# A forward-and-backward adaLN block on one Trainium2 core: the 2048-point transform split as 16 x 128 instead of 128 x 16

## The chip, the cores and the metric

The kernel runs on one core of a Trainium2 chip. The metric is the device time of one launch in microseconds (us); lower is better. The engines are TensorE (PE; its weight loads are listed apart as PEld), VectorE (DVE), ScalarE (ACT), GpSimd (POOL) and SyncE (SP). DMAs are issued from SP's queue and from POOL's.

## The reference

The block computes an output and the gradients of all its inputs but one, for 2048 rows of width 576 in bfloat16:

```
mod = silu(c) @ w_mod                     # sa, ca, ga, sb, cb, gb, 576 each
h = layernorm(x) * (1 + ca) + sa
X = rfft2(h)                              # over 2048 rows and 576 columns, 289 frequencies kept
y = irfft2(X * (w_r + 1j * w_i))
x = x + ga * y
h = layernorm(x) * (1 + cb) + sb
x = x + gb * (((h @ w_gate) * (h @ w_up)) @ w_down)     # hidden width 4608
# outputs: x, and the vjp for grad_out: x, w_r, w_i, w_gate, w_up, w_down, c, w_mod
```

The two-dimensional transform is needed once forward (h to y) and once backward (gradient of y to gradient of h, with the filter's gradient from both spectra).

## The kernel before

The 2048 rows are cut into 16 blocks of 128, row 16 p + t in partition p of block t. The columns' transform is a product with a table (RD forward, RF on folded rows backward). The transform of 2048 rows is split: within a block over the 128 partitions with the twiddled table G1, then across the 16 blocks.

**Head, first stage** (`s1_norm`, `s1_cols`, `s1_rows`; three steps of a software pipeline over the blocks). A block is normalised, transposed on PE (five products of 128 columns, L473), multiplied by the scaled table RDs (ten of 292, L482) and by G1 (four of 292, L502 and L503), and its planes are copied to VA. Meanwhile grad_out is transposed on PE (L532) and scaled by DVE into goT (L535).

**Head, second stage** (`s2_*`, 19 chunks of up to four groups out of 73). A group holds four frequencies of all 16 blocks. For each group PE transposes it (L599), multiplies with BD2, the 16-point transform as a block-diagonal table (L607), DVE multiplies by the filter wn (L238) and adds, PE transposes back (L628) and multiplies with BDA (L636). ACT and DVE copy each result out of PSUM. Between the steps `u4_groups` puts two groups of the ghh product (`u4_group`, L572: five matmuls of 512 columns each, 144 groups in all), and the last three modulators (`mod_make`).

**Head, third stage** (`s3_*`, 16 blocks). `rows_back` (L210, L212) multiplies the planes with the twiddled table GB, `cols_back` (L217) with IF, the halves are folded (L219 to L221), the residual and the second norm follow. Three groups of ghh go between, the rest after.

**Middle.** The gated products forward and backward and the weight gradients, over 36 hidden blocks (L757, L840, L879).

**Tail, first stage** (`t1_*`, 16 blocks): backward through the second norm, a PE transpose (L1166), twelve narrow matmuls for the modulators' diagonals (`diag`, L1053), six with RF (L1181) and four with G1 (L1188, L1189). **Second stage** (`t2_*`): the same 19 chunks as in the head. **Third stage** (`t3_*`): `rows_back`, `cols_back`, the first norm backward. `filter_grad` forms the filter's gradient from the kept spectrum Xn on DVE (L1290 to L1295), `product_rows` the rows of the w_mod gradient (L1095).

The order on PE in the tail is written out by hand. `staged` keeps the matmuls of every step; `deal` puts a fixed number `q` of other matmuls behind each step: the last weight gradients (`held`) and the first five pairs of output tiles (`proj`, L1464), 896 in all, and ties the whole into one chain with `in_order`. ACT's order in the first tail stage, and ACT's and DVE's in the third, are tied likewise. In the head a planner orders the work by priorities and costs. PSUM has eight banks: in the head five for `fps` and three for `u4ps`; in the tail three for `ps_fp`, three single ones for `ps_cs` (csA, csB, csC) and two for `ps_u3`. An engine takes its instructions in order, so one that waits holds all behind it.

## Time and profile before

| | us |
|---|---|
| median of 3 runs | 1499.98 |
| lowest and highest | 1499.88, 1500.52 |
| profiled execution | 1497.33 |
| its span | 1495.6 |
| PE busy | 1476.1 (99%) |
| DVE busy | 1057.9 (71%) |
| ACT busy | 566.9 (38%) |
| POOL busy | 255.0 (17%) |
| granted TensorE clock, mean | 0.998 |

The profile is one execution. A line of a group names the kernel's line, the engine, the operation, output and inputs by tile, the shapes and the count; then the busy time and the mean duration in ns of one; then the idle time of the engine just before these instructions and what ended most of it. A line of the timeline starts with its start in us and its length. Matmuls are pipelined and their ends are modelled, so that a row of ten lasts from its start to the start of the next row.

### The profile page before, as it was taken

What the parts mean: (1) busy time and instruction counts of PE and PEld (TensorE: products, weight loads), DVE (VectorE), ACT (ScalarE), POOL (GpSimd) and SP (SyncE); (2) the same over time, 40 slices, a digit from 0 to 9 for tenths busy, and PEclk for the clock granted to TensorE, in tenths of its full rate; (3) what the DMA queues carried; (4) which work ended last, traced back from release to release, by engine and by line L of the source; (5) the groups of instructions that cost most, each with busy time, mean ns of one, the idle gap of its engine ahead of it and who ended that gap; (6) DMA issues with size and microseconds to landing.
All of it is one profiled execution on the core that took longest, in us unless ns stands there. A gap on an engine that the chain in (4) does not pass through costs nothing.

```text
span 1495.6 us, 29166 instructions
## 1 busy us (share of the span) xinstructions
PE 1476.1 (99%) x11249; PEld 1009.5 (68%) x11251; DVE 1057.9 (71%) x2648; ACT 566.9 (38%) x1186; POOL 255.0 (17%) x396
## 2 busy tenths in 40 slices
...
GB/s 323 274 224 212 241 224 187 155 152 168 161 138 181 138 127 180 134 139 183 128 143 185 117 146 177 124 150 174 124 155 142 132 141 295 266 262 193 245 312 149
DMA packets 486350, 272.92 MB, mean 182 GB/s; under 512 B 413921, under 2 KB 457186, under 8 KB 485186
## 3 DMA queue, kind: packets, MB, share of 16 engines
...
## 4 chain that ended last, share of the span: by engine, by line
PE 91%; DMA 3%; issue 2%; DVE 2%; POOL 1%; SPq 1%; ACT 0%; POOLq 0%; DVEq 0%; ACTq 0%
PE u57p L757 27%; PE u8p L879 19%; PE gup L840 17%; PE u4p L572 10%; PE u3p L1464 5%; PE gup L835 3%; PE yp L217 1%; PE u57p L791 1%; DMA gonA<-in_grad_out_dram 1%; DMA h2p<-in_A_x_dram 1%; PE zp L1181 1%; PE upa L210 1%; PE zp L482 1%; DMA gxc<-gx_d 1%; PE u4p L567 0%
## 5 line engine op out<-in xcount | busy, mean ns | idle before, releaser
L884 DVE TENSOR_TENSOR acc<-acc,u8p 128x288 f32<-128x288 f32 (+1 forms) x1088 | 483.0, 452 | 276.2 <-PE u8p L879 272.5
L879 PE MATMUL u8p<-wT,ggT 128*128 128x288 bf16 x1152 | 327.8, 286 | 0.7 <-DVE acc L884 0.7
L879 PE MATMUL u8p<-wT,guT 128*128 128x288 bf16 x1152 | 327.5, 286 | 0.0
L840 PE MATMUL gup<-h2T,wgu 128*128 128x512 bf16 x1152 | 297.8, 379 | 0.0
L759 ACT CAST so<-u57p 128x288 bf16<-128x288 f32 x208 | 82.9, 399 | 510.9 <-PE u57p L757 505.3
L757 PE MATMUL u57p<-h2p,gu_sf 128*128 128x288 bf16 x1088 | 176.6, 286 | 0.0
L757 PE MATMUL u57p<-h2p,gg_sf 128*128 128x288 bf16 x1088 | 176.6, 286 | 0.0
L840 PEld LDWEIGHTS <-wgu 128*128 128x128 bf16 x1152 | 109.6, 98 | 97.9 <-issue 17.1
L879 PEld LDWEIGHTS <-ggT 128*128 128x128 bf16 x1152 | 112.6, 98 | 66.9 <-issue 14.5
L572 PE MATMUL u4p<-goT,wdT 128*128 128x512 bf16 x668 | 153.8, 379 | 0.0
L879 PEld LDWEIGHTS <-guT 128*128 128x128 bf16 x1152 | 112.7, 98 | 56.1 <-issue 0.9
L1464 PE MATMUL u3p<-wd,hl 128*128 128x288 bf16 x936 | 140.1, 286 | 0.5 <-ACT ob L1469 0.5
L842 ACT CAST gT<-gup 128x512 bf16<-128x512 f32 x144 | 84.4, 586 | 131.5 <-PE gup L840 129.6
L757 PEld LDWEIGHTS <-hh_sf 128*128 128x128 bf16 x1152 | 112.7, 98 | 28.4
L1464 PEld LDWEIGHTS <-hl 128*128 128x128 bf16 x1152 | 107.5, 98 | 26.6 <-issue 3.4
L757 PEld LDWEIGHTS <-gu_sf 128*128 128x128 bf16 x1088 | 106.5, 98 | 27.0
L757 PEld LDWEIGHTS <-gg_sf 128*128 128x128 bf16 x1088 | 106.5, 98 | 26.8
L842 ACT CAST uT<-gup 128x512 bf16<-128x512 f32 x144 | 84.4, 586 | 77.5 <-PE gup L840 77.5
L572 PEld LDWEIGHTS <-wdT 128*128 128x128 bf16 x668 | 62.5, 98 | 70.9 <-issue 5.5
L757 PE MATMUL u57p<-gonC,hh_sf 128*128 128x288 bf16 x576 | 99.7, 286 | 0.0
L855 POOL DMA_DIRECT2D hhT_d<-hhT x36 | 33.2, 923 | 373.8 <-DVE hhT L844 373.2
L169 ACT CAST ghh_st<-u4p 128x512 bf16<-128x512 f32 x94 | 53.7, 589 | 53.6 <-PE u4p L572 52.9
...
## 6 DMA issues: line engine op xcount, KB each, us to landing
...
```

The lines of the kernel that those rows point to most:

```text
L169: nc.scalar.copy(dst, src)
L210: nc.tensor.matmul(ps_a[:, fc, :], lhsT=A[:, c, sa, 128 * fc:128 * fc + 128], rhs=GB[:, sa, 1 - c:3 - c, :].rearrange("k v s -> k (v s)"), ...
L572: nc.tensor.matmul(pt[:], lhsT=wdTs[k][:, j, m, :], rhs=goT[:, 4 * sb4:4 * sb4 + 4, m, :], start=(m == 0 and n == 5), stop=(m == n - 1))
L757: mm = nc.tensor.matmul(pw[0][:, 0:288], lhsT=sf[:, t, :], rhs=rhs_n(t, h * 288, 288), start=(t == 0), stop=(t == NT - 1))
L759: followed(mm, nc.scalar.copy(so[:, h * 288:(h + 1) * 288], pw[0][:, 0:288]))
L835: nc.tensor.matmul(pts[-1][:], lhsT=wgu[r, 8, jw * 128:(jw + 1) * 128], rhs=h2T[r, 4 * sb4:4 * sb4 + 4, 4, :], start=True, stop=False)
L840: nc.tensor.matmul(pts[k][:], lhsT=wgu[:, 4 * wi_ + m, jw * 128:(jw + 1) * 128], rhs=h2T[:, ts_, m, :], start=False, stop=(m == 3))
L842: nc.scalar.copy((gT, uT)[wi_][:, th_, :], pts[k][:])
L855: nc.gpsimd.dma_start(hhT_d[:, :, fb, :].rearrange("tp f x -> f tp x"), hhT[:].rearrange("f (tp ti) p -> f tp (ti p)", ti=2))
L879: nc.tensor.matmul(pu[:, 0:288], lhsT=l_, rhs=r_, start=(k == 0), stop=(k == len(mms) - 1))
L884: summed[t] = nc.vector.tensor_tensor(out=ghb(t)[:, hs_] if fbs[-1] == NFB - 1 else dst, in0=dst, in1=pu[:, 0:288], op=ADD).ins
L1464: mm = nc.tensor.matmul(p2[ti][:, 0:288], lhsT=hls[fb // 9][:, fb % 9, ti * 128:(ti + 1) * 128], rhs=w[:, fb - f0, h * 288:(h + 1) * 288], ...
```

## The change

The split is turned round: 16 points first, within one turned block, then 128 points.

- The turn of a block is a matmul with the table F16 in place of the identity (`turn16`): it turns the block and takes the 16-point transform of it at once. The result goes to h2T (head) or GY (tail), real and imaginary lanes side by side. The 73 group turns and products with BD2, and those back with BDA, are gone, and VA, Vp and the planes A with them.
- Lanes i and 16 - i are made as a pair (eight pairs, the last holding lanes 0 and 8). `freq_rows` takes four results of two matmuls each from the pair's columns with G1, `both_signs` makes both lanes from their sums and differences (two copies on ACT, four DVE operations), `spectral_product` multiplies by the filter and forms sums and differences again, `plane_back` goes back over 128 points with GB.
- `cols_back` now comes before `rows_back`, which is a matmul with I16 (F16 transposed) on each half.
- The column part (RD, RF) moves from the first stages into the second. The head's first stage keeps the norm, the turn and grad_out's transposes; ghh groups, modulators and the turn of the first two w_down blocks on PE lie between them by a written order. The loads on SP are reordered; the turned half of the filters is read through a DRAM copy (back_d).
- In the tail `deal` gives 24, 12 and 17 matmuls a step (before 16, 12 and 16); the second norm's last affine and the product rows go from DVE to ACT; the filter gradient is taken by lane (16 in place of 19), eight of them in the third stage; G1, GB and I16 are loaded in the first stage; half of the filter gradient's store goes through a DRAM copy (gback_d).

```diff
+    p = 16 * (q % 8) + q // 8
+    th = 2 * np.pi * p[:, None, None] * (16 * k1[None, None, :] + k2[None, :, None]) / S
     G1 = np.stack([np.cos(th), -np.sin(th), np.sin(th)], axis=2)
-    thp = 2 * np.pi * (q[:, None, None] * (16 * k1[None, None, :] + t[None, :, None])) / S
+    thp = np.transpose(th, (2, 1, 0))
     GB = np.stack([-np.sin(thp), np.cos(thp), np.sin(thp)], axis=2)
...
+    F16 = np.zeros((128, 128), f8)
+    for j in range(NT):
+        kk = j // 2 if j > 1 else 8 * j
+        w = np.cos(2 * np.pi * np.arange(NT) * kk / NT) if j % 2 == 0 or j == 1 else -np.sin(2 * np.pi * np.arange(NT) * kk / NT)
+        for l in range(8):
+            F16[8 * np.arange(NT) + l, 8 * j + l] = w
...
+    def lane(i, u):
+
+        return i if u == 0 else NT - i if i else NPR
+    def turn16(src, dst, t, room, tag):
+        pts = [room.tile([128, 4, 128], FP32, name="tr16", tag=tag) for _ in range(2)]
+        for m in range(5):
+            mm = nc.tensor.matmul(pts[m // 4][:, m % 4, :], lhsT=src(m), rhs=T["F16"][:], start=True, stop=True)
+            if m > 2:
+                n = 4 if m == 3 else 1
+                followed(mm, nc.scalar.copy(dst[:, :, m + 1 - n:m + 1, 8 * t:8 * t + 8].rearrange("q j m l -> q m j l"), pts[m // 4][:, 0:n, :].rearrange("q m (j l) -> q m j l", l=8)))
+    def freq_rows(G, zt, i, new):
+        ps = [new() for _ in range(4)]
+        ar, ai, br, bi = (zt[:, a, c, :] for a in range(2) for c in range(2))
+        for p_, (k, terms) in zip(ps, ((i, ((0, ar), (2, br))), (i, ((0, bi), (1, ai))), (i, ((0, ai), (2, bi))), (i, ((0, br), (1, ar)))) if i else
+                                  ((0, ((0, ar), (2, ai))), (0, ((0, ai), (1, ar))), (NPR, ((0, br), (2, bi))), (NPR, ((0, bi), (1, br))))):
+            for n, (pl, z) in enumerate(terms):
+                nc.tensor.matmul(p_[:, 0:FP], lhsT=G[:, k, pl, :], rhs=z, start=(n == 0), stop=(n == 1))
+        return ps
+    def both_signs(ps, i, X, pool):
+        if i == 0:
+            for n, p_ in enumerate(ps):
+                nc.scalar.copy(X[:, n // 2, n % 2, :], p_[:, 0:FP])
             return
+        es = pool.tile([128, 2, FP], FP32, name="es", bufs=1)
+        for n in range(2):
+            nc.scalar.copy(es[:, n, :], ps[2 * n][:, 0:FP])
+            for u, op in ((n, SUB), (1 - n, ADD)):
+                nc.vector.tensor_tensor(out=X[:, u, n, :], in0=es[:, n, :], in1=ps[2 * n + 1][:, 0:FP], op=op)
+    def spectral_product(X, wn, i, sd, nrest, pool, conj):
+        m1 = pool.tile([128, 2, 2, 2, FP], BF, name="fm", bufs=1)
+        for c in range(2):
+            nc.vector.tensor_tensor(out=m1[:, c], in0=X, in1=wn[:, c, lane(i, 0):lane(i, 1) + 1:lane(i, 1) - lane(i, 0), :].unsqueeze(2).to_broadcast([128, 2, 2, FP]), op=MUL)
+        Y = m1[:, 0].rearrange("k u c f -> k (u c) f")
+        for c in range(2):
+            nc.vector.tensor_tensor(out=m1[:, 0, :, c, :], in0=m1[:, 0, :, c, :], in1=m1[:, 1, :, 1 - c, :], op=ADD if conj == (c == 0) else SUB)
+        for f0, w, at in ((0, FM, 0), (FM, FP - FM, 2 * FM)):
+            dst = [sd[:, e, at:at + 2 * (FM if at == 0 else 64)].rearrange("k (c f) -> k c f", c=2)[:, :, 0:w] for e in range(2)]
+            if i:
+                nc.vector.tensor_tensor(out=dst[0], in0=y[:, 0:2], in1=y[:, 2:4], op=ADD)
+                nc.vector.tensor_tensor(out=dst[1], in0=y[:, 1:3], in1=y[:, 3::-3], op=SUB)
...
+    def plane_back(GB, sd, i, nrest, ut, new):
         for fc in range(2):
+            ps = new()
+            for e in range(2):
+                for n in range(2):
+                    a, c, k = (n, e, i) if i else (e, n, NPR * e)
+                    nc.tensor.matmul(ps[:, 256 * e:256 * e + 256], lhsT=sd[:, a, FM * c + 128 * fc:FM * c + 128 * fc + 128], rhs=GB[:, k, 1 - n:3 - n, :].rearrange("k v s -> k (v s)"), start=(n == 0), stop=(n == 1))
...
+            for e in range(2):
+                nc.scalar.copy(dst[:, e], ps[:, 256 * e:256 * e + 256].rearrange("f (v s l) -> f v s l", v=2, l=8))
+        ps = new()
...
+        nc.scalar.copy(ut[:, 4, :, 16 * i:16 * i + 16].rearrange("f s (u l) -> f u s l", l=8), ps[:, 0:256].rearrange("f (u s l) -> f u s l", u=2, l=8))
+    def cols_back(ut, t, yps, IF, pool):
         for p_, pls in enumerate(((0, 2, 4), (1, 3, 4))):
             for k, pl in enumerate(pls):
+                nc.tensor.matmul(yps[p_][:, 0:DF], lhsT=ut[:, pl, t, :], rhs=IF[:, 3 * p_ + k, :], start=(k == 0), stop=(k == 2))
+            made.append(nc.scalar.copy(zz[:, p_, :], yps[p_][:, 0:DF]).ins)
+    def rows_back(zz, yps, I16, pool, out):
+        for p_ in range(2):
+            nc.tensor.matmul(yps[p_][:, 0:DF], lhsT=I16, rhs=zz[:, p_, :], start=True, stop=True)
...
-        PE_TURNED = (13, 15, 17)
+        PE_TURNED = (0, 1, 13, 15, 17)
...
+        T = {"F16": load_table(hp1, "F16")}
         x_load(0, 1)
-        wms[MCA] = mod_load(MCA)
-        T = {"RD": load_table(hp1, "RD", "tA")}
+        wms[MGB] = mod_load(MGB)
         go_load(0)
         wd_load(0)
+        x_load(4, 8)
+        go_load(1)
         x_load(8, 12)
         go_load(2)
         x_load(12, NT)
+        wms[MCA] = mod_load(MCA)
+        T["RD"] = load_table(hp1, "RD", "tA")
+        T["G1"] = load_table(hp1, "G1")
+        for c, filt in enumerate((wr_v, wi_v)):
+            nc.sync.dma_start(back_d[c].rearrange("k j f -> j k f"), turned_rows(filt))
...
+        gate()
+        s1_norm(0)
+        pe_turn(0)
+        s1_stats(1)
+        s1_stats(2)
+        for t in range(1, NT):
+            if t in (4, 6, 8, 12):
+                s1_stats(t)
+            s1_norm(t)
+            go_turn(t - 1)
+            if t == 5:
+                pe_turn(1)
+                mod_make(MGB, wms[MGB], "a")
+                wms[MSA] = mod_load(MSA)
+            if t == 13:
+                shift_row()
+            if t == 7:
+                scaled_table()
+            if t == 9:
+                mod_make(MCA, wms[MCA])
+                wd_ready(2)
+                wms[MGA] = mod_load(MGA)
+            if t in (4, 6, 8, 9, 10, 11, 12, 13, 14):
+                u4_groups(1)
+        go_turn(NT - 1)
+        nc.gpsimd.memset(wn[:, :, :, DF:FP], 0.0)
+        for c, filt in enumerate((wr_v, wi_v)):
+            nc.sync.dma_start(wn[:, c, 0:NPR + 1, 0:DF], filt[:, 0:NPR + 1, :])
+            nc.sync.dma_start(wn[:, c, NPR + 1:NT, 0:DF], back_d[c])
+        nc.gpsimd.dma_start(wn_d, wn[:].rearrange("k c a f -> k (c a f)"))
+        for k_ in ("GB", "I16"):
+            T[k_] = load_table(hp1, k_)
+        for j in (MGA, MSB, MCB):
+            u4_groups(2)
+            mod_make(j, wms.get(j) or mod_load(j), "a")
...
+                ps = freq_rows(T["G1"], zts[n], i, new)
+                X = Xs[n] = c2.tile([128, 2, 2, FP], BF, name="Xc")
+                both_signs(ps, i, X, c2)
+                nc.sync.dma_start(xn_d[:, i * W4:(i + 1) * W4], X[:].rearrange("k u c f -> k (u c f)"))
...
+            for k in range(NPR + 3):
+                if k > 2:
+                    s2_back(k - 3)
+                    u4_groups(1)
+                if 1 < k < NPR + 2:
+                    s2_filter(k - 2)
+                if 0 < k < NPR + 1:
+                    s2_rows(k - 1)
+                    u4_groups(1)
+                if k < NPR:
+                    s2_cols(k)
+                if k == 0 or k >= NPR:
+                    u4_groups(2)
+            in_order(pe_since(mark))
...
-        pipeline(NT, [lambda sa: (s3_rows(sa), u4_groups(3, "a")), s3_cols, s3_norm])
+        pipeline(NT, [lambda sa: (s3_cols(sa), u4_groups(3, "a")), s3_rows, s3_norm])
...
-            if name == "1":
-                nc.scalar.activation(out=part(w), in_=part(n), func=ACT.Identity, bias=ab[:, 0:1], scale=ab[:, 1:2])
-            else:
-                nc.vector.tensor_scalar(out=part(w), in0=part(n), scalar1=ab[:, 1:2], scalar2=ab[:, 0:1], op0=MUL, op1=ADD)
+            scaled["w" + name].append(nc.scalar.activation(out=part(w), in_=part(n), func=ACT.Identity, bias=ab[:, 0:1], scale=ab[:, 1:2]).ins)
...
-                q = 16 if stage == 1 else 12 if stage == 2 else 20 if k == 0 else 16
+                q = 24 if stage == 1 else 12 if stage == 2 else 20 if k == 0 else 17
...
-            nc.vector.tensor_scalar(out=o8[r, m, :], in0=d[r, :], scalar1=sc_col[r, m:m + 1], scalar2=None, op0=MUL)
+            nc.scalar.activation(out=o8[r, m, :], in_=d[r, :], func=ACT.Copy, scale=sc_col[r, m:m + 1])
...
+                        for tab, tag, at in (("RF", "tA", 10), ("G1", None, 11), ("GB", None, 13), ("I16", None, 14)):
+                            if t == at:
+                                T[tab] = load_table(tl0, tab, tag)
+                                in_order([ins.ins, tab_ins[tab]])
...
-                for m in range(5):
-                    mm = nc.tensor.transpose(pt[:, m, :], rings["gxf"][:, t % 3, wide(m)], ident[:])
+                turn16(lambda m: rings["gxf"][:, t % 3, wide(m)], GY, t, ps_fp, "fp")
...
-            steps = [t1_norm, t1_turn, t1_cols, t1_last]
+            steps = [t1_norm, t1_out, t1_turn, t1_last]
...
+        def filter_grad(g):
+            i, u, s_ = g // 2, g % 2, lane(g // 2, g % 2)
+            Xn = fg.tile([128, 2, FP], BF, name="Xn2")
...
+            for c in range(2):
+                nc.vector.scalar_tensor_tensor(out=t1[:, c], in0=Xn[:, c, :].unsqueeze(1).to_broadcast([128, 2, FP]), scalar=CSC, in1=gY(i)[:, u], op0=MUL, op1=MUL)
+            nc.vector.tensor_tensor(out=wn[:, 0, s_, :], in0=t1[:, 0, 0, :], in1=t1[:, 1, 1, :], op=ADD)
+            nc.vector.tensor_tensor(out=wn[:, 1, s_, :], in0=t1[:, 0, 1, :], in1=t1[:, 1, 0, :], op=SUB)
...
-            pipeline(NCH, [t2_turn, t2_filter, None, t2_back, t2_inv, t2_grad], 2)
+            def new_cs():
+                turn[0] += 1
+                return ps_cs.tile([128, 512], FP32, name="fq", tag="cs" + "ABC"[turn[0] % 3])
+                        for m in range(3):
+                            nc.tensor.matmul(zp[:, 0:FP], lhsT=GY[:, 2 * i + a, 2 * cc + m, :], rhs=T["RF"][:, 3 * cc + m, :], start=(m == 0), stop=(m == 2))
+                        nc.scalar.copy(zt[:, a, cc, :], zp[:, 0:FP])
+            def t2_rows(n):
+                both_signs(freq_rows(T["G1"], zts[n], pairs[n], new_cs), pairs[n], gY(pairs[n]), c2)
+            def t2_filter(n):
+                spectral_product(gY(pairs[n]), wn, pairs[n], sds[n % 2], nrest, c2, True)
+            def t2_back(n):
+                plane_back(T["GB"], sds[n % 2], pairs[n], nrest, utB, new)
+            pipeline(NPR, [t2_cols, t2_rows, t2_filter, t2_back], 2)
...
+        T["IF"] = load_table(tl0, "IF", "tA", nc.gpsimd)
...
-            ut = uts[sa] = c3.tile([128, 640], BF, name="ut", bufs=3)
-            own["ut", sa] = [nc.scalar.copy(ut[:, 0:512], upa[:].rearrange("f c s -> f (c s)")).ins, nc.scalar.copy(ut[:, 512:640], upb[:, 0:128]).ins]
-            ye, *own["fold", sa] = cols_back(uts[sa], [ps_fp.tile([128, 512], FP32, name="yp", tag="fp") for _ in range(2)], T["IF"], c3, ghr3[:, sa % 3, :])
+            ye, *own["fold", sa] = rows_back(zzs[sa], [ps_fp.tile([128, 512], FP32, name="yp", tag="fp"), ps_cs.tile([128, 512], FP32, name="yp", tag="csB")], T["I16"][:], c3, ghr3[:, sa % 3, :])
...
-            if sa in (4, 7, 10, 13):
-                filter_grad(rest[sa // 3 - 1])
+            if sa % 2:
+                filter_grad(rest[sa // 2])
...
-        pipeline(NT, [t3_rows, t3_cols, t3_norm, t3_sums], 3)
+        pipeline(NT, [t3_cols, t3_rows, t3_norm, t3_sums], 3)
...
-            for ci in rest[{9: 4, 10: 6, 11: 8}.get(t, 99):][:2]:
+            for ci in rest[{9: 8, 10: 12}.get(t, 99):][:4]:
...
+                    if t == 8:
+                        nc.gpsimd.dma_start(gback_d[c], wn[:, c, NPR + 1:NT, 0:DF])
+                    if t == 9:
+                        nc.gpsimd.dma_start(turned_rows(o_v), gback_d[c].rearrange("k j f -> j k f"))
+                if t == 11:
+                    scale_ends(0, NPR + 1)
+                for k in {11: range(2), 12: range(2, 4), 13: range(4, 6)}.get(t, ()):
+                    nc.gpsimd.dma_start((o2_v, o3_v)[k % 2][:, 3 * (k // 2):3 * (k // 2) + 3, :], wn[:, k % 2, 3 * (k // 2):3 * (k // 2) + 3, 0:DF])
 
```

500 lines of the change are left out of this document (167 added, 333 removed).

## The prediction

> **What bounds the kernel now.** I read the page first (busy time by engine), then the stage table for the stretches that the change touches, then TensorE's timeline inside them, and last the groups by line for durations on VectorE (DVE) and ScalarE (ACT).
>
> ```profile
> PE 1476.1 (99%) x11249; PEld 1009.5 (68%) x11251; DVE 1057.9 (71%) x2648; ACT 566.9 (38%) x1186; POOL 255.0 (17%) x396
> ```
>
> ```profile
> 0.00:14.00 14.00, 10.21 (x126) 8.98 (x126) 6.51 (x35) 7.00 (x12) 3.58 (x16) 1.00 0.80 268
> 14.00:16.00 2.00, 0.60 (x6) 0.60 (x7) 1.77 (x9) 1.16 (x2) 0.00 (x0) 0.86 0.99 392
> 16.00:18.00 2.00, 2.00 (x10) 1.08 (x9) 1.53 (x6) 1.50 (x2) 0.00 (x0) 0.50 1.06 392
> 18.00:20.00 2.00, 1.81 (x15) 1.17 (x13) 1.74 (x7) 1.73 (x5) 0.19 (x1) 0.78 1.06 384
> 20.00:64.20 44.20, 41.63 (x428) 31.89 (x427) 25.39 (x69) 30.55 (x77) 5.17 (x7) 1.00 0.97 312
> 64.20:130.30 66.10, 66.10 (x535) 40.02 (x533) 47.51 (x139) 42.89 (x86) 7.52 (x14) 1.00 0.71 213
> 1243.00:1313.50 70.50, 70.45 (x741) 58.18 (x740) 55.82 (x157) 56.27 (x134) 24.60 (x37) 1.00 0.88 284
> 1313.50:1367.70 54.20, 53.66 (x597) 45.78 (x595) 47.52 (x134) 43.81 (x93) 12.09 (x27) 1.00 0.59 193
> 1367.70:1432.20 64.50, 63.82 (x601) 52.24 (x601) 57.62 (x167) 46.92 (x111) 17.89 (x32) 1.00 0.81 255
> ```
>
> The columns are the stretch in us, its length, the busy time of PE, PEld, DVE, ACT and POOL, the granted clock, the DMA share and GB/s. Six rows are the stages in question: the forward transform's column part (to 64.2), its spectral part (to 130.3), then the three tail stages. In the last four PE is idle for 1.3 us in all. So TensorE is the bound wherever the change works, except before about 20 us, and a matmul taken away is time taken away as long as nothing else is late. The margins are thin: in the first tail stage DVE is busy for 55.82 and ACT for 56.27 of 70.50 us.
>
> PE's busy time is modelled, so I take prices from start to start.
>
> ```profile
> 114.00 0.39 PE L607 MATMUL xp<-T_BD,VT 128*128 128x128 bf16 x4
> ...
> 114.89 2.32 PE L572 MATMUL u4p<-goT,wdT 128*128 128x512 bf16 x10
> 117.05 0.39 PE L607 MATMUL xp<-T_BD,VT 128*128 128x128 bf16 x4
> ```
>
> ```profile
> 1286.83 0.44 PE L1166 MATMUL trp<-ident,gxf 128*128 128x128 bf16 x5
> ...
> 1287.63 1.14 PE L1464 MATMUL u3p<-wd,hl 128*128 128x288 bf16 x8
> 1288.61 0.29 PE L1188 MATMUL vp<-zt,T_G 128*128 128x292 bf16 x1
> ...
> 1289.11 0.65 PE L1464 MATMUL u3p<-wd,hl 128*128 128x288 bf16 x4
> ```
>
> ```profile
> 1417.15 0.60 PE L210 MATMUL upa<-T_GB,j_A 128*128 128x256 bf16 x4
> 1417.59 0.28 PE L212 MATMUL upb<-T_GB,j_At 128*128 128x128 bf16 x2
> 1417.70 0.65 PE L1464 MATMUL u3p<-wd,hl 128*128 128x288 bf16 x4
> ```
>
> One chunk of the spectral part is four groups of four narrow matmuls, 114.00 to 114.89: 0.89/16 = 0.056 us each. Ten of the ghh product's matmuls with 512 columns take 2.16 us, 0.216 each, so a group of five is 1.08. A fill matmul of 288 columns is 0.98/8 = 0.1225. Four of 292 columns take 0.50 (0.125 each). Five transposes with twelve diagonal matmuls take 0.80. Of 256 columns one is 0.11, of 128 again 0.055.
>
> **The change part by part: TensorE.** Removed: the turn, the 16-point product, the second turn and the second product of 73 column groups, so 4 x 73 = 292 narrow matmuls in each direction, 584 in all: 584 x 0.056 = 32.7 us. Added: two matmuls of 289 columns with the I16 table for each of 16 row blocks in each direction, 64 x 0.125 = 8.0 us. Two more blocks of w_down are turned on PE instead of by DMA: 20 x 0.056 = 1.1 us. Same count and width, only moved: the turn by F16 (five of 128 per block, as the transposes), the column part (160 and 96 of 292), the row part (64 of 292 each way), the way back (64 of 256 and 32 of 128, now 78 and 4, the same columns). Net: 8.0 + 1.1 - 32.7 = -23.6 us of PE work, of which the tail has -12.4 and the head -11.2 (4.0 + 1.1 - 16.4). The 20 warm-up matmuls at 12 us go too; they lay in a wait, so nothing. This is all gain only if no new wait appears.
>
> **Who takes over: durations.**
>
> ```profile
> L1290 DVE SCALAR_TENSOR_TENSOR gwt<-Xn,b_Vp 128x512 f32<-128x512 bf16 x36 | 24.2, 683 | 0.1
> ...
> L238 DVE TENSOR_TENSOR fm<-b_Vp,wn 128x512 bf16<-128x512 bf16 x36 | 13.6, 419 | 5.9 <-ACT b_Vp L1316 5.9
> ...
> L535 DVE TENSOR_TENSOR goT<-u4p,gbT 128x640 bf16<-128x640 bf16 x16 | 12.7, 815 | 14.0 <-PE u4p L532 14.0
> L181 DVE BATCH_NORM_STATS2 ln_st<-h2p 128x6 f32<-128x288 bf16 x32 | 12.7, 436 | 4.4 <-DMA h2p<-in_A_x_dram 4.4
> ...
> L220 DVE TENSOR_TENSOR ghr<-yp,ye 128x289 bf16<-128x289 f32 x16 | 7.3, 455 | 0.0
> ...
> L1322 DVE TENSOR_TENSOR Ygc<-fm 128x256 bf16<-128x256 bf16 x18 | 5.1, 285 | 0.3
> ```
>
> ```profile
> L1016 ACT ACTIVATE w<-n1c,ab 128x576 bf16<-128x576 bf16 x16 | 14.1, 881 | 0.3 <-DVE ab L1010 0.3
> ...
> L169 ACT COPY hT<-trp 128x640 bf16<-128x640 bf16 x16 | 11.1, 693 | 1.1 <-PE trp L473 1.1
> ...
> L1371 ACT CAST ut<-upa 128x512 bf16<-128x512 f32 x16 | 9.4, 589 | 9.2 <-PE upa L210 9.2
> ...
> L1371 ACT CAST ut<-upb 128x128 bf16<-128x128 f32 x16 | 4.4, 275 | 0.0
> ```
>
> Each row ends with busy us and mean ns. Neighbours overlap a little: 36 times 419 ns is 15.1 us, but the row was busy 13.6, so sums of means come out about 10% high. From 256 to 512 columns a bf16 product grows by 134 ns, 0.52 ns a column on a base of 0.15 us. A column pair then costs DVE: four signed sums from PSUM at 0.455 = 1.82; two products of 1168 columns at 0.76, two sums of 584 at 0.46, two of 512 at 0.42, two of 72 at 0.19 = 3.66; together 5.5 us, about 5.0 with the overlap. ACT: six copies of 292 columns (between 0.275 and 0.589, by width 0.41) and five of 256 (0.38) = 4.4 us.
>
> **Head, first stage.** With the column part gone from it, PE has here only 80 turns and 80 transposes of grad_out (9.0 us), two modulators and the shift row (30 matmuls of 288 to 292 columns, 3.7), the modulators' columns (80 matmuls of one column, an estimate of 2 to 4 from the 0.056 of 128), w_down (1.1) and nine ghh groups (9.7): some 26 us. So PE no longer sets its length. DVE does: it is busy 36.9 us to 64.2 (6.51 + 1.77 + 1.53 + 1.74 + 25.39), of which 25.4 are the statistics and the scaled copies of grad_out, which stay. What leaves is six plane copies of 292 columns (0.455 each by the row of ghr), six norms and two copies of ghh (0.4 to 0.6 each by the same rows), 6 us; what comes is four copies of w_down of 640 columns, 2 to 3 us at no more than goT's 0.794. That makes some 33 us. It starts at about 5 us and waits for x at times: the stage ends at 43. Six ghh groups and three modulators follow (6 x 1.08 + 3 x 1.23 = 10.2): 54 us is the lower end for the spectral part's start. The upper end is the DMA: by 64.2 us the queues have moved 0.268 x 14 + 0.392 x 4 + 0.384 x 2 + 0.312 x 44.2 = 19.9 MB, and the new order wants about as much before that point: x, grad_out, w_down, the filters and the stores of n1 as before; earlier than before GB (it was loaded after the spectral part) and three modulators; in addition a DRAM copy of the filters' turned half; but G1 and GB are 9/16 as large. At the measured rate that is 60 to 63 us. On SP's queue the last modulator's load stands behind the filter loads and GB, and the third modulator product waits for it. I take 58, between the ends, since the loads that PE needs first (x, grad_out) go out first now.
>
> **Head, spectral part.** A pair costs PE 28 x 0.125 + 10 x 0.11 = 4.6 us; with 24 ghh groups eight pairs make 62.7 us. A step with two ghh groups is 6.76; DVE needs 5.0 and ACT 4.4 of it, each and one ghh copy of 512 columns (0.59 by the row of ut): PE holds it. I add 2 us for the first and last pair. It ends at 58 + 65 = 123 against 130.3, with 39 ghh groups made instead of 42, 3.2 us still owed: -4.1. In the third stage each of 16 blocks costs 0.25 for I16 and no longer the 0.55 of the way back: -4.8. Head: -8.9, with ends -13 (start at 54) and -4 (at 63).
>
> **Tail.** The 896 fill matmuls (the last weight gradients and the first five output tile pairs, dealt between the steps, 109.8 us) stay; 16, 12 and 16 a step become 24, 12 and 17. First stage: a step is PE 0.80 + 24 x 0.1225 = 3.74 us in place of 4.01. ACT has two norms and w, moved there from DVE (576 columns, 0.88 each by the w row), two turn copies (0.59 + 0.275, formerly one of 0.693) and two thirds of a fill copy (0.27): 3.8 by means, 3.4 with overlap. So about 70 us as now, but 152 fills further. Second: eight pairs 28.8 + 132 fills 16.2 = 45.0 us of PE in place of 54.2; DVE at 5.0 of 5.07 us a pair has no slack, the last pair's way back must land before the next stage's first matmul, and the tail's row part has four results for three banks (csA, csB, csC): 3 to 8 us lost, I take 4. Third: 326 fills and 16 x (8 x 0.125 + 0.27) make 60.2 us of PE. ACT gets 20 product rows there, formerly DVE's, of 576 columns, so 0.88 us by the nearest row: w and u (0.88), ye and two zz (0.41) and half a fill copy are 3.2 a step, with these rows 16 x 3.2 + 17.6 = 69 us, 62 with overlap. DVE loses those rows but has eight filter gradients of 2 x 0.76 + 2 x 0.46 = 2.4 us instead of four. I take 2.5 us of loss, with 0 and 8 as ends. After it nothing changes: 432 output matmuls cover what is left, and the filter stores number ten instead of 16. Tail: -12.4 + 4 + 2.5 = -5.9, ends -12 and +4.
>
> **Sum.** The profiled execution took 1497.3 us, 1.7 more than its span, and 2.7 less than the median of 1499.98. 1497.3 - 8.9 - 5.9 = 1482.5 there, 1485 for the median.
>
> **The clock: row against rule.** From 14 to 16 us PE is idle for 1.4 of 2 us, and in the two after that the granted clock is 0.50. The new first stage gives PE 26 us of work in 43, in many short gaps. If it ran at half clock throughout, its 26 us would be 52, the spectral part would start at 5 + 52 + 10 = 67 instead of 58, and the time be 1494. The Trainium skill, "TensorE: Matmul & The Clock Gate", Part 1, says the clock falls to half after an idle window of about 3.4 us and rises after as long of sustained work. By that rule the short gaps would not lower it and the head's term stays as summed. The row is harsher than the rule: 1.4 us of idling in a stretch of two came before the fall.
>
> **The rivals.** (1) All of the PE work is gained, the new waits being covered: 1500 - 23.6 = 1476. For it: four stages with 1.3 us idle. Against it: the DVE and ACT sums above. (2) The gain is mostly eaten in two places, the late modulator in the head (-4) and ACT or DVE in the tail's third stage (-2): 1494. (3) The half clock in the head, also 1494, and 1501 if it lasts through the first pair (6.8 us more). (4) Slower: the pairs run at the pace of their own chain. Rows need four PSUM banks at once, freed only when DVE has made the signed sums, and PE takes its instructions in order, so a late bank holds the ghh and fill matmuls behind it. If the 1.82 us of sums stand bare in each of 16 pairs, that is 29 us: 1485 + 29 - 6 (the losses counted) = 1508. It decides from 1.3 us a pair on, (15 + 6)/16. Against it: now, too, each chunk passes PE, ACT, DVE, PE, ACT, PE, with idle of 0.5 us in 54.2.
>
> **How the numbers follow.** My case (1479 to 1491) 0.45, (1) 0.15, (2) 0.18, (3) 0.07, (4) 0.15. This kernel's measurement tells about 0.2%, 3 us, from no change. Faster: 0.45 + 0.15 + 0.13 of (2) and 0.03 of (3), 0.76; within it the rest of (2) and 0.03 of (3), 0.08; slower (4) and 0.01 of (3), 0.16. The range reaches from just under (1) to between (3) and (4): 1474 to 1503; my case's own is 1479 to 1491.
>
> **What would show it.** Right: no narrow 128-column groups in the spectral parts; pairs every 6.8 us in the head and 5.1 in the tail; the spectral part starting at 54 to 63 us. Wrong: PE idle released by DVE's signed sums or by the banks csA to csC, PE waiting on a modulator load near 55 us, a granted clock under 1 past 20 us, or ACT at 95% in the third tail stage with PE waiting for zz.

## The result and the profile after

The changed kernel takes 1552.49 us (median of four runs, 1549.55 to 1557.08) against 1499.93 before (1498.01 to 1500.52): 1.0355 times the time, 95% interval 1.0328 to 1.0383. The prediction was 1485, and the range 1474 to 1503 does not hold it. The profiled execution took 1549.55, its span is 1546.5, 50.9 more than before.

The first fence is the page's busy time by engine, the second the stage table of the changed kernel, cut at the same places as that of before; its columns are those of the prediction.

```profile
PE 1460.5 (94%) x10701; PEld 987.6 (64%) x10703; DVE 1049.7 (68%) x2576; ACT 558.7 (36%) x1191; POOL 248.4 (16%) x393
```

```profile
0.00:72.08 72.08, 49.69 (x451) 34.53 (x452) 34.81 (x116) 36.33 (x78) 10.51 (x27) 0.83 0.95 313
72.08:264.67 192.59, 191.55 (x1111) 102.16 (x1109) 121.55 (x281) 110.35 (x251) 30.18 (x57) 1.00 0.71 203
264.67:1255.67 991.00, 989.54 (x7106) 669.26 (x7106) 696.39 (x1651) 257.77 (x508) 140.15 (x187) 1.00 0.73 149
1255.67:1338.12 82.45, 66.59 (x689) 54.83 (x687) 44.37 (x133) 51.66 (x108) 19.48 (x40) 0.94 0.84 283
1338.12:1385.38 47.26, 46.32 (x377) 36.11 (x375) 40.87 (x107) 32.59 (x94) 5.96 (x11) 1.00 0.33 115
1385.38:1450.00 64.62, 55.39 (x483) 42.68 (x482) 55.90 (x151) 49.85 (x112) 16.36 (x29) 1.00 0.71 218
1450.00:1520.10 70.10, 61.37 (x498) 48.01 (x496) 44.36 (x117) 19.59 (x40) 16.53 (x28) 0.95 0.78 232
1520.10:1546.50 26.40, 0.02 (x1) 0.00 (x0) 11.47 (x26) 0.57 (x1) 9.22 (x16) 0.57 0.37 89
```

The rows of before that answer to these and were not shown yet:

```profile
0.00:64.20 64.20, 56.26 (x579) 43.73 (x580) 36.95 (x122) 41.93 (x96) 8.94 (x23) 0.97 0.94 310
64.20:259.47 195.27, 195.25 (x1260) 103.41 (x1257) 123.93 (x307) 115.75 (x234) 33.37 (x61) 1.00 0.79 220
259.47:1246.37 986.90, 985.95 (x7074) 666.13 (x7073) 694.88 (x1647) 255.85 (x504) 138.02 (x184) 1.00 0.76 151
1246.37:1313.50 67.13, 67.08 (x714) 55.58 (x713) 52.45 (x148) 55.87 (x133) 22.20 (x35) 1.00 0.86 285
1432.20:1488.70 56.50, 54.00 (x442) 42.66 (x439) 43.90 (x125) 6.22 (x16) 21.96 (x34) 1.00 0.81 252
1488.70:1495.60 6.90, 0.04 (x1) 0.00 (x0) 0.60 (x3) 0.57 (x1) 0.55 (x1) 0.84 0.19 40
```

Length less PE's busy time is PE's idle time, so the two tables (with the two tail rows in the prediction) give the whole account, in us:

| stretch | length before, after | PE busy, change | PE idle before, after |
|---|---|---|---|
| start to the first pair's column product | 64.2, 72.1 | -6.6 | 7.9, 22.4 |
| to the middle | 195.3, 192.6 | -3.7 | 0.0, 1.0 |
| middle, to the tail's first turn | 986.9, 991.0 | +3.6 | 1.0, 1.5 |
| first tail stage | 67.1, 82.5 | -0.5 | 0.1, 15.9 |
| second | 54.2, 47.3 | -7.3 | 0.5, 0.9 |
| third, and the outputs to PE's last matmul | 121.0, 134.7 | -1.1 | 3.2, 18.0 |
| after PE's last matmul | 6.9, 26.4 | 0 | 6.9, 26.4 |
| sum | 1495.6, 1546.5 | -15.6 | 19.5, 86.0 |

(The middle is 4 us longer because 32 more matmuls stand in it, 7106 for 7074; as dealt ones of 288 columns they are worth 32 x 0.1225 = 3.9.) The work was saved; 66.5 us of new idle time stand against it, in four places. PE's waits, by what they wait for, in the tail:

```profile
PE u3p L1458 <- DMA hl<-hhT_d: 12.0, 2, 10.8
PE spp L1100 <- DVE dca L1085: 7.8, 2, 7.2
PE u3p L1458 <- ACT ob L1463: 6.9, 5, 2.4
```

Columns are us in total, times, the longest. None of the tail's waits is on the signed sums or on the banks csA to csC; only 0.8 us is for `sd`, the sums after the filter.

The head, from the timelines of PE and of SP's queue:

```profile
65.49 2.56 PE L398 MATMUL modps<-wm,sc_rep 128*128 128x288 bf16 x10 [6.47 <-DMA wm<-in_w_mod_dram]
```

```profile
0.73 0.38 SPq L302 DMA_DIRECT2D T_GB<-tab_GB  x1
...
50.68 0.39 SPq L612 DMA_DIRECT2D wn<-in_A_w_r_dram  x1
...
57.53 0.73 SPq L390 DMA_DIRECT2D wm<-in_w_mod_dram  x1
```

The last modulators' loads are issued at 57.53 us, behind the filter loads, and PE waits 6.47 us for the first. GB's table, which the program lists behind the filters, is issued first of all, at 0.73 us, ahead of x.

The first tail stage, POOL's timeline:

```profile
1286.58 0.98 POOL L1242 DMA_DIRECT2D wd<-in_B_w_down_dram  x1 [7.05 <-DMA T_RF<-tab_RF]
1287.55 0.58 POOL L1242 DMA_DIRECT2D hl<-hhT_d  x1
...
1300.00 0.55 POOL L1188 DMA_DIRECT2D gx_d<-gxr  x1 [10.27 <-DVE gxa L1190]
```

One load of w_down (`wd`) holds the queue for 7.05 us before it can start (what ends this wait is read from the runs below); the load of `hl` behind it starts at 1287.55, and PE, whose output matmuls come every step in the written order, waits 10.82 for an `hl` until 1293.97. Then no step of the stage can run (POOL's next store waits 10.27 for DVE).

The end, DVE's timeline. PE's last matmul ends at 1520.1:

```profile
1487.06 0.76 DVE L1128 SCALAR_TENSOR_TENSOR pr<-wmj,dcb 128x576 bf16<-128x576 bf16 x1 [9.90 <-DMA wmj<-in_w_mod_dram]
...
1520.66 1.43 DVE L1294 SCALAR_TENSOR_TENSOR gwt<-Xn,b_GY 128x584 f32<-128x584 bf16 x2
```

The last filter gradients stand in DVE's order behind and among the sums with w_mod (`pr`), which themselves began 9.90 us late. Their scaling and stores follow on POOL.

### The profile page after: what moved, and what is told of

Read it like the earlier page. It is cut to its first block, busy times and chain, and to the rows that moved or that the text cites. A ratio compares the mean times of both kernels' runs of the same rounds, so it can differ in the third digit from the quotient of the medians.

```text
span 1546.5 us, 27857 instructions
## 1 busy us (share of the span) xinstructions
PE 1460.5 (94%) x10701; PEld 987.6 (64%) x10703; DVE 1049.7 (68%) x2576; ACT 558.7 (36%) x1191; POOL 248.4 (16%) x393
## 5 line engine op out<-in xcount | busy, mean ns | idle before, releaser
L1458 PE MATMUL u3p<-wd,hl 128*128 128x288 bf16 x936 | 134.7, 289 | 20.1 <-DMA hl<-hhT_d 12.0
L1458 PEld LDWEIGHTS <-hl 128*128 128x128 bf16 x1152 | 111.7, 99 | 64.6 <-issue 23.7
L169 ACT CAST ghh_st<-u4p 128x512 bf16<-128x512 f32 x102 | 58.2, 585 | 72.3 <-PE u4p L574 69.1
```

Source lines behind the costliest of these rows:

```text
L169: nc.scalar.copy(dst, src)
L1458: mm = nc.tensor.matmul(p2[ti][:, 0:288], lhsT=hls[fb // 9][:, fb % 9, ti * 128:(ti + 1) * 128], rhs=w[:, fb - f0, h * 288:(h + 1) * 288], ...
```

## The experiments

The theory: the saved PE work is real; four things ate it, the head's bytes, POOL's queue in the first tail stage, the written orders of the tail's third stage, and DVE's order at the end. The rivals are named in the expectations. In all ratios the kernel before was run beside. All times of landmarks are from the profiled execution of each run.

### Deal of the fill matmuls: fills16

```diff
-                q = 24 if stage == 1 else 12 if stage == 2 else 20 if k == 0 else 17
+                q = 16 if stage == 1 else 12 if stage == 2 else 25
```

> The fill matmuls are dealt 16, 12 and 25 a step instead of 24, 12 and 17; nothing else differs. Theory A (the fills run ahead of their own loads in the first tail stage, and the third has too little work to cover ScalarE): the 10.8 us wait for hl goes, TensorE's idle time in the first stage falls from 17 us to under 4, the eight more fills a step (0.98 us) fill the third stage's gaps, and the time falls from 1552 to about 1530. Rival B (both stages are held by ScalarE's and VectorE's own work, the wait for hl only lies inside it): the first stage keeps its 80 us, the third gets 18.6 us longer, 1552 to 1570.

1544.94 us, 1.0311 (1.0290 to 1.0331). The wait for `hl` is gone, another stands in its place. PE's waits in the first tail stage, then POOL's:

```profile
PE tr L197 <- DVE gxf L1191: 10.7, 4, 10.0
```

```profile
POOL wd L1242 <- DMA yc<-y_d: 12.8, 1, 12.8
```

The `wd` load now holds POOL's queue for 12.8 us, until 1295.00. The smaller deal spreads the last weight gradients' matmuls over more steps, until 1288.0, and the second part of the store of one of these gradients (`woT`) is issued at 1288.71 and lands 5.6 us later, 0.7 us before the load starts. The gx stores behind it stop, then DVE, which has no free gxr, then PE's turn. The hold is what stays. The stage took 68.6 us, not 82.5, with a third fewer fills. The time lies between what the two theories had named (1530, and 1552 or more).

### The first output tiles' loads earlier: hlearly

```diff
-        for t, *loads in ((1, (0, 7)), (2, 0), (3, (7, 7)), (4, (14, 7)), (5, 1), (6, (21, 7)), (7, (28, 7), 2), (8, (35, 1), 3)):
+        for t, *loads in ((1, (0, 7), 0), (2, (7, 7)), (3, (14, 7), 1), (4, (21, 7)), (5, 2, (28, 7)), (6, 3, (35, 1))):
```

> The loads of the first output pair and of w_down are queued two to three blocks earlier; the deal stays 24, 12, 17. Theory A (late loads): the wait for hl goes and the time falls by 11 to 14 us, to about 1540. Rival B (ScalarE and VectorE hold the stage): within 4 us of 1552.

1553.91 us, 1.0372 (1.0348 to 1.0396): nothing gained, 9.94 us of the wait stay. The time is that of rival B, but the trace does not show its reason: the `wd` load holds POOL's queue for 13.51 us, until 1291.04, and the last `hl` load still goes out behind it, at 1293.12.

### The modulators' loads ahead of the filters: wmearly

```diff
-wm = pool.tile([128, 5, D], BF, name="wm")
+wm = pool.tile([128, 5, D], BF, name="wm", bufs=3)
...
                 shift_row()
+                for j in (MSB, MCB):
+                    wms[j] = mod_load(j)
```

> The loads of the last two modulators go out before the filters', with a third buffer. Theory A (TensorE waits for a modulator that stands behind the filters on SP's queue): the 6.5 us wait and the half clock after it go, the spectral part starts at 64 instead of 72 us, 1544. Rival (the DMA engines are full until about 70 us, so that the filters or GB come late instead): a wait of 5 to 8 us before the first spectral product or the first way back, 1550 to 1553.

1553.63 us, 1.0373 (1.0351 to 1.0395). The pairs begin at 63.45 in place of 72.08, but the third stage at 135.71 in place of 134.95. PE's waits in the pairs, then DVE's:

```profile
PE fq L644 <- DVE Xc L222: 7.9, 1, 7.9
```

```profile
DVE Xc L222 <- DMA xn_d<-Xc: 10.2, 1, 10.2
```

The store of an early pair's spectrum is late in a full DMA, and holds the next pair's signed sums and then PE. The 8 us were handed on, as the rival said.

### The filters' loads ahead of w_down's: headq

wmearly's edit, and the filter loads moved up to stand before `wd_ready(2)`:

```diff
             if t == 9:
                 mod_make(MCA, wms[MCA])
...
+                for c, filt in enumerate((wr_v, wi_v)):
+                    nc.sync.dma_start(wn[:, c, 0:NPR + 1, 0:DF], filt[:, 0:NPR + 1, :])
+                    nc.sync.dma_start(wn[:, c, NPR + 1:NT, 0:DF], back_d[c])
                 wd_ready(2)
```

> As the run with the early modulators, and the filters' four loads go out before the third block of w_down, whose transposing DMA held SP's queue from 41.7 to 48.4 us while the DMA engines were not full. Theory A (order on SP's queue): the spectral part starts at 64 us, the 7.9 us wait of its first signed sums for VectorE goes, the third stage starts at 127 instead of 135, 1544. Rival (the DMA engines must move some 24 MB before the first pair is filtered, in whatever order): something else of the head comes late, the third stage starts at 133 to 136, 1550 to 1553.

1557.85 us, 1.0392 (1.0376 to 1.0407): PE waits 10.5 us for a modulator again, the pairs begin at 78.0, the third stage at 140.9. An order of the same loads moves the wait about; it doesn't remove it.

### Fewer bytes in the head: headlean

wmearly's edit; the DRAM copy of the filters' turned half is left out and that half is loaded unturned (so the turn of these rows is left out of the computation), and GB's load is listed later:

```diff
-            nc.sync.dma_start(back_d[c].rearrange("k j f -> j k f"), turned_rows(filt))
...
-            nc.sync.dma_start(wn[:, c, NPR + 1:NT, 0:DF], back_d[c])
+            nc.sync.dma_start(wn[:, c, NPR + 1:NT, 0:DF], filt[:, NPR + 1:NT, :])
```

> As the run with the early modulators; in addition the turned half of the filters is loaded as it lies, without the DRAM copy (that half of the filters then stands in the wrong rows: the turn is left out), and GB is loaded after the filters and w_down. 2 MB less go through the DMA engines before the first pair. Theory A (the head waits for bytes, not for their order): at 390 GB/s 2 MB are 5 us, the spectral part starts at 63 to 64 us, the 7.9 us wait of the signed sums falls to under 3, the third stage starts at 128 to 130, 1545. Rival (the order on the queues, or ScalarE and VectorE in the first pairs): 133 to 136 as before, 1550 to 1553.

1545.7 us, 1.0302 (1.0283 to 1.0321). The pairs begin at 63.24, the third stage at 128.34, 6.6 earlier than in the changed kernel. GB's load was issued near 0.7 us all the same, wherever the program lists it, so what was taken off is the copy alone.

### The same with the whole computation: wnlate_gbhold

wmearly's edit; GB's load tied behind the filter loads, and the store of the padded filters (`wn_d`, 128 x 2 x 16 x 292 values of 2 bytes, 2.4 MB) held until the fifth pair:

```diff
-        nc.gpsimd.dma_start(wn_d, wn[:].rearrange("k c a f -> k (c a f)"))
...
+            in_order([filt_in, tab_ins[k_]])
...
+                if k == 4:
+                    in_order([stored[-1], nc.gpsimd.dma_start(wn_d, wn[:].rearrange("k c a f -> k (c a f)")).ins])
```

> The head alone: modulators early, the load of GB (0.9 MB, issued at 0.7 us) held back behind the filters, and the store of the filters for the tail (2.4 MB at 64 us) held back until the fifth pair. The turn of the filters is kept. Theory A (bytes bound the head): 3.2 MB less before the first pair are 8 us at 390 GB/s; the third stage starts at 126 to 129 in place of 135, 1544. Rival (VectorE and the chain of the first pairs bound it): 133 to 136, 1551.

1545.87 us, 1.0329 (1.0268 to 1.0390; one run of 1564.07 widens it). The interval tells no difference from 1.0355, but the trace shows the place: pairs from 64.26, third stage at 127.36, 7.6 earlier, with PE waiting 0.2 us in all of the pairs.

```profile
0.00:64.26 64.26, 47.87 (x451) 34.97 (x452) 35.03 (x116) 35.77 (x78) 9.74 (x26) 0.87 0.96 294
```

The first row of the changed kernel has moved 72.08 x 313 = 22.6 MB by the same point, this one 64.26 x 294 = 18.9 MB, at a DMA share of 0.95 and 0.96. Two reorderings (wmearly, headq) gained nothing, two reductions or delays of bytes 6.6 and 7.6 us: the head is bound by the DMA. headlean alone would not tell this, since without the copies SP's queue is also free of their issues (0.92 and 10.33 us long in the changed kernel), and it had moved 63.24 x 332 = 21.0 MB by its first pair. wnlate_gbhold keeps the copies, so that it speaks for the bytes that are due.

### The half clock: warm

Three times 24 matmuls of warm-up within the first 25 us:

```diff
         gate()
+        warm_up(24)
         s1_norm(0)
...
             go_turn(t - 1)
+            if t in (2, 3):
+                warm_up(24)
```

> 72 warm-up matmuls are put into TensorE's gaps of the first 25 us; nothing else differs. If the half clock from 12 to 28 us costs time, the clock is 1.00 from about 15 us on and the spectral part starts 3 us or more earlier, 1548. If VectorE and the loads set the pace there, the start stays at 72 us and the time within 3 us of 1552.

1557.86 us, 1.0377 (1.0354 to 1.0399). One row of the changed kernel, then of this one:

```profile
14.00:28.00 14.00, 8.17 (x58) 5.86 (x56) 12.43 (x40) 8.22 (x20) 1.67 (x2) 0.50 1.06 387
```

```profile
14.00:28.00 14.00, 8.60 (x94) 7.99 (x92) 10.19 (x33) 7.08 (x17) 0.91 (x1) 0.76 1.05 386
```

The clock rose from 0.50 to 0.76 there, and the pairs began at 76.7, later still, with PE waiting 8.5 us for a modulator (6.47 in the changed kernel). With the DMA share at 1.05 and 1.06 the higher clock brought the start no forward; why it came 4.6 us later is not settled.

### POOL's hold released earlier: fills16_wotearly, and with the tables later: fills16_wotearly_tablate

fills16's edit, and the store of `woT` (the last but one weight gradient) at step 9 in place of 12; in the second kernel also RF, G1, GB and I16 loaded at the steps 13 to 15:

```diff
-            for t, k in zip((5, 6, 12, NT), range(4)):
+            for t, k in zip((5, 6, 9, NT), range(4)):
...
-                        for tab, tag, at in (("RF", "tA", 10), ("G1", None, 11), ("GB", None, 13), ("I16", None, 14)):
+                        for tab, tag, at in (("RF", "tA", 13), ("G1", None, 14), ("GB", None, 15), ("I16", None, 15)):
```

> As the run with 16, 12 and 25 fills a step, and the store of the turned weight gradient woT stands three blocks earlier on SP's queue. Theory A (a load of w_down on POOL's queue waits for that store, and the stores of gx behind it hold VectorE and so all): the 10 us wait at 1308 us goes, 1545 becomes about 1535. Rival (DMA engines at 400 GB/s hold the stage): a wait of over 6 us stays in the first tail stage, 1541 to 1547.

> As the run with 16, 12, 25 fills and the earlier store, and the tables RF, G1, GB and I16 are loaded with blocks 13 to 15 in place of 10 to 14, so that 1.8 MB leave the stretch from 1270 to 1300 us in which the DMA engines move 380 GB/s without a pause. Theory A (bytes hold the first tail stage): its 11 us of waits fall to 4 to 7, the time from 1544.6 to about 1539. Rival (POOL's queue behind the w_down load): the waits stay at 10 us or more, 1543 to 1546, or the second stage now waits for its tables.

1544.57 us, 1.0296 (1.0278 to 1.0315), and 1548.38, 1.0309 (1.0286 to 1.0332), fills16 being 1.0311. The waits for gxf stay (7.4 and 6.3 us), and POOL's `wd` load still waits 11.31 (until 1288.49) and 11.21 (until 1293.97). The store has long landed now (12.5 us after its issue at 1270.30 in the first). What the load starts behind, by 0.3 us in both kernels, is the end of the last dealt weight-gradient matmul, 1288.18 and 1293.67. So two things end the hold, these matmuls and the store of `woT` (both still read memory that the load goes into, by these times), and the later one counts: the earlier store alone hands the wait to the matmuls. The tables are not among them.

### More of them early, fewer late: wotearly_deal2

```diff
-                q = 24 if stage == 1 else 12 if stage == 2 else 20 if k == 0 else 17
+                q = (24 if k < 7 else 12) if stage == 1 else 12 if stage == 2 else 25
```

with the store at step 9 as above.

> The first tail stage alone: woT's store three blocks earlier, and 24 fills a step only until the last weight gradient's products are through (7 steps), then 12, with 25 a step in the third stage. Theory A (the w_down load waits for the memory that these products read, and POOL's queue behind it holds the rest): the product ends at 1277, POOL's wait falls from 7 to 13 us to under 3, TensorE's waits in the stage from 17 us to under 6, 1541. Rival (the DMA engines, full from 1266 to 1300 us): 10 us of waits stay, 1545 or more.

1549.41 us, 1.0320 (1.0298 to 1.0342). The first stage takes 65.6 us with fewer fills, but POOL's load still waits 7.69, until 1287.38, PE 7.6 for `hl` and 4.8 for ACT's GY, as the rival on record had it. Now the matmuls are done at 1276.5, and it is the store again: its second part is issued at 1270.72 and lands 15.9 us later, at 1286.6, while the DMA moves 320 GB/s from 1266 to 1300. The line of the store in this run, and the `wd` load's wait in headlean, which deals as the changed kernel does and where the profile names the store itself:

```profile
out_dram<-woT SPq DMA_DIRECT2D x1, 32.0 KB, 15.9
```

```profile
POOL wd L1242 <- DMA out_dram<-woT: 9.8, 1, 9.8
```

In the changed kernel the last of the matmuls ends at 1276.35, ten us before the load starts (1286.58), and the store's second part is issued at 1280.51; no landing of it is recorded there, but in the trace of the DMA engines the last of its 576 packets of 512 bytes ends at 1285.5. So there, too, the late store is what the load waits for. No run gives the store more room with nothing else changed.

### The product rows' place and memory: rowsdve, rowsroom

rowsdve puts the 576-column rows back on DVE; rowsroom gives the last ones a buffer of their own, so that ACT makes them earlier (at 1477.56 in place of 1498.26, 20.7 us; 27 were expected):

```diff
-            nc.scalar.activation(out=o8[r, m, :], in_=d[r, :], func=ACT.Copy, scale=sc_col[r, m:m + 1])
+            nc.vector.tensor_scalar(out=o8[r, m, :], in0=d[r, :], scalar1=sc_col[r, m:m + 1], scalar2=None, op0=MUL)
```

```diff
-                o8s[j] = tl.tile([128, 5, D], BF, name="o8")
+                o8s[j] = (secp if j == MSA else tl).tile([128, 5, D], BF, name="o8s" if j == MSA else "o8", bufs=1)
```

> Only the product rows go back to VectorE, 0.32 us each by the kernel before in place of 0.71 on ScalarE. If ScalarE holds the third tail stage, it shortens by 6 to 10 us, and the time is about 1544. If VectorE holds it (10.0 of 10 us busy from 1400 to 1420), 20 rows make it 4 to 7 us longer, 1557.

> The last product rows get a buffer of their own, so that ScalarE makes them some 27 us earlier. Theory A (their store holds POOL's queue, and behind it stand the loads for the last filter gradients): what follows TensorE's last matmul falls from 26.6 us to 8 to 14, the time to about 1538. Rival (VectorE has too much to do after 1470 us, the six sums of w_mod and eight gradients, whatever the queue does): 24 us or more stay, within 4 us of 1552.

rowsdve: 1547.29 us, 1.0327 (1.0303 to 1.0352), some 4 us better, at the edge of what the intervals tell; PE's waits for ACT's `ob` fall from 6.9 to 2.1. rowsroom: 1553.17, 1.0355 (1.0333 to 1.0378), no gain. PE still ends 27.2 us before the span, because the gradients follow the w_mod sums in DVE's order:

```profile
POOL Xn L1291 <- DVE gs L1491: 33.9, 1, 33.9
```

### The gradients first: gradsfirst

rowsroom's edit; the remaining filter gradients at the steps 7 and 8, ahead of the sums, and gback's store two steps later:

```diff
-            for ci in rest[{9: 8, 10: 12}.get(t, 99):][:4]:
+            for ci in rest[{7: 8, 8: 12}.get(t, 99):][:4]:
...
-                    if t == 8:
+                    if t == 10:
                         nc.gpsimd.dma_start(gback_d[c], wn[:, c, NPR + 1:NT, 0:DF])
```

> Only the end: the last eight filter gradients are put two blocks earlier, ahead of the six sums of w_mod on VectorE, the DRAM copy of the stored half two blocks later, and the last product rows have a buffer of their own. Theory A (order on VectorE and POOL's queue): what follows TensorE's last matmul falls from 26.6 us to 8 to 11, 1552 becomes about 1535. Rival (VectorE has over 48 us of work after 1470 us in any order): 18 us or more stay, 1543 or above.

1537.11 us, 1.0248 (1.0219 to 1.0278): 15 us recovered of 52. The time after PE's last matmul falls from 26.4 to 7.0, and the wait for dca from 7.2 to 1.3; the edit has three parts, of which only the buffer was run by itself (rowsroom, no gain). What is late next is DVE's sums themselves, and PE's last matmul with them:

```profile
PE gcp L1499 <- DVE gcd L1495: 10.9, 1, 10.9
```

### Together: all_orders, best

all_orders joins fills16, the store at step 9, gradsfirst, rowsdve and wmearly. best joins wnlate_gbhold, wotearly_deal2, gradsfirst and rowsdve, and issues the last residual loads from SP:

```diff
-                x1l = nc.gpsimd.dma_start(x1t[:], x1_d[:, 2 * tp_:2 * tp_ + 2, :])
+                x1l = (nc.gpsimd if tp_ < 5 else nc.sync).dma_start(x1t[:], x1_d[:, 2 * tp_:2 * tp_ + 2, :])
```

> The orders that helped, together: 16, 12, 25 fills, the earlier store of woT, the filter gradients ahead of the w_mod sums, the product rows on VectorE, the modulators early. If the waits are separate places on one chain, the gains add: 1552 - 8 - 15 - 5 = 1524. If they only hand the wait on (VectorE gets the rows just where the gradients stand), 1532 or more. Under 1500 by neither theory, since the first 70 us and the first tail stage stay bound by bytes.

> Both of these, with the filter gradients ahead of the w_mod sums, the product rows on VectorE, and the last residual loads on SP's queue in place of POOL's. If the waits are separate: 1530 - 8 (head) - 8 (first tail stage) - 10 (end, where the last residual load came 8 us late) = 1504. If they hand each other the wait, 1515 or more. The predicted 1485 is out of reach for either.

all_orders: 1530.0 us, 1.0195 (1.0176 to 1.0215); DVE waits 8.4 us at the end for a residual load that stands behind gback's stores on POOL's queue. best: 1515.52, 1.0102 (1.0087 to 1.0117), 37 us less than the changed kernel, 15 more than before. Its stage table:

```profile
0.00:62.46 62.46, 46.49 (x452) 33.67 (x452) 35.04 (x116) 35.85 (x78) 9.81 (x26) 0.89 0.94 301
...
1247.49:1307.61 60.12, 49.14 (x544) 41.21 (x543) 42.19 (x127) 46.08 (x98) 18.73 (x33) 0.91 0.91 315
1307.61:1359.65 52.04, 48.08 (x377) 36.76 (x374) 41.24 (x107) 32.91 (x95) 4.27 (x13) 0.97 0.37 119
...
1501.92:1513.70 11.78, 0.00 (x0) 0.00 (x0) 1.36 (x6) 0.51 (x1) 1.86 (x3) 0.50 0.53 99
```

PE is busy for 1457.1 us, 19.0 less than before, and idle for 56.6, 37.1 more. Half of that lies in the head (16.0, before 7.9) and the first tail stage (11.0, before 0.1), a quarter in the second stage and the end (4.0 and 11.8, before 0.5 and 6.9). In the end POOL's queue waits twice for gback's DRAM store, 6.31 us the first time:

```profile
1485.24 1.13 POOL L1430 DMA_DIRECT2D out_dram<-gback_d  x1 [6.31 <-DMA gback_d<-wn]
```

Set against the changed kernel's ratio of 1.0355, the four parts of best that ran singly are worth some 4 us (wnlate_gbhold), 5 (wotearly_deal2), 16 (gradsfirst) and 4 (rowsdve), 29 in sum, and best with its moved residual loads 37 to 38. But 1504 was on record for waits that are separate and 1515 or more for waits that hand each other on, and 1515.52 is the second. No version here beats the kernel before.

## Why the prediction was wrong

**PE's work: right, a third too large.** -23.6 was predicted, -15.6 measured; best has -19.0. The pieces hold: a pair starts every 6.73 us in the head (predicted 6.76) and every 5.25 in the tail (5.1), a block of the third stage every 4.24 (4.54 less 0.30 predicted, 4.24), the pairs' part takes 62.9 us (65), the second tail stage 47.3 (45.0 + 4).

```profile
110.67 2.65 PE L642 MATMUL fq<-RDs,h2T 128*128 128x292 bf16 x20
117.40 2.65 PE L642 MATMUL fq<-RDs,h2T 128*128 128x292 bf16 x20
```

```profile
1357.97 1.66 PE L1322 MATMUL fq<-T_RF,b_GY 128*128 128x292 bf16 x12
1363.22 1.66 PE L1322 MATMUL fq<-T_RF,b_GY 128*128 128x292 bf16 x12
```

The 8 us missing are of the size of the half-clock stretches that the new waits bring. If a matmul at a low clock takes longer in proportion, the rows above and below give 8.17 x 0.50 = 4.1 (14 to 28 us), 6.03 x 0.42 = 2.5 and 6.00 x 0.30 = 1.8, together 8.4, an estimate; the rows of before from 14 to 20 us give 1.5 by the same sum. It does not fit place by place: 5.9 of the 8.4 lie in the head, where 10.3 of the 11.2 us forecast were saved, while the rest of the kernel saved 5.3 of 12.4. So most of the shortfall of the tail stays unexplained.

```profile
66.00:72.00 6.00, 6.00 (x29) 3.21 (x28) 0.33 (x1) 1.97 (x4) 0.55 (x1) 0.70 1.09 414
...
1290.00:1300.00 10.00, 6.03 (x43) 4.61 (x44) 1.37 (x5) 2.75 (x6) 0.00 (x1) 0.58 0.63 229
```

**Head, first stage: the step that failed is "at the measured rate that is 60 to 63 us" as an upper end, and 58 as the value.** The DMA was named as the bound, but the bytes were taken as "about as much before that point"; by the start of the pairs 22.6 MB had moved, not 19.9. The items it named there were put at nothing: by the sizes of their issues in the traces GB, three modulators and the copy, less what G1 shrank by, are 0.9 + 2.2 + 1.0 - 0.7 = 3.4 MB, some 11 us at 310 GB/s, an estimate. Where the pairs began earlier (63.45 us and 19.5 MB in wmearly), the rest was paid inside them. Also wrong was where GB stands: not behind the filters on SP but at the head of the queue. The start was 72.08; 14 us of that term. The modulator's load, which rival (2) had at 4 us, was the place where it showed, 6.47 us; headq, headlean and wnlate_gbhold show that the load's place is not the cause.

**First tail stage: "so about 70 us as now" failed.** It took 82.5. The step counted PE, DVE and ACT, all of which would have fitted, and charged nothing to the queues, although the deal makes the first output tiles due earlier: 24 fills a step call for `hl` while the `wd` load in front of it on POOL's queue still waits. 15.8 us of PE idle follow. That the hold on POOL's queue is in the chain is shown by fills16 (it moves to gxf). What ends the hold is the later of the last dealt weight-gradient matmul and the landing of the store of `woT`, by the times of the runs above; no edit freed it by itself (the store, the tables, the deal). In best POOL waited 2.40 us for it (the store landed 10.7 us after its issue, not 15.9), and the stage took 60.1 with fewer fills.

**Third tail stage: "2.5 us of loss, with 0 and 8 as ends" failed.** 14.8 more idle. ACT's rows were sized at 0.88 and are 0.78, so ACT is not the reason by its sum; 4 us went when DVE took them back. The larger wait, 7.24 us at 1466.31, was in no term: the store of `ob` of the last block but two lands 9.84 us after its issue at 1455.67, between two gback stores and beside six `hl` loads, DVE can't write the next `ob`, and dca stands behind that on DVE. The chain that ended last, then POOL's timeline and DVE's, of the changed kernel:

```profile
1455.67 9.84 DMA out_dram<-ob
```

```profile
1454.84 0.99 POOL L1424 DMA_DIRECT2D gback_d<-wn  x1
1455.67 0.74 POOL L1390 DMA_DIRECT2D out_dram<-ob  x1
1456.21 1.16 POOL L1424 DMA_DIRECT2D gback_d<-wn  x1
```

```profile
1465.63 0.46 DVE L1040 TENSOR_TENSOR ob<-u,w 128x576 bf16<-128x576 bf16 x1 [7.39 <-DMA out_dram<-ob]
1466.00 0.25 DVE L1085 TENSOR_TENSOR dca<-csE,ident 128x96 bf16<-128x96 f32 x1
```

In gradsfirst, where gback's store comes two steps later, PE's wait for dca is 1.3 us.

**"After it nothing changes" failed, and is the largest term that one edit recovers.** 432 output matmuls do cover what is left on PE, but six of the last eight filter gradients stood among or behind the w_mod sums in DVE's order. 19.5 us more after PE's last matmul; gradsfirst, which moves them ahead (and gback's store behind), took 15 us off the whole.

**The rivals.** (4) did not happen in the changed kernel: no wait for signed sums or banks (in wmearly there was one of 7.9 us, which a late store set off). (3) happened in the records (clock 0.50 from about 12 to 28.6 us); warm, which raised the clock in part of that stretch, gives no sign that it set the start of the pairs. (2) named a right place with a wrong price, but nothing as large as this sum. What was missing is a rival in which the removed matmuls had been the cover of the loads.

The Trainium skill, "TensorE: Matmul & The Clock Gate", Part 1, lets the clock fall after an idle window of about 3.4 us. The trace went another way than the prediction read that rule: the row from 12 to 14 us has 0.50, behind a gap of 2.55 us and in or behind one of 2.00, and none longer had come; after it the gaps were 0.82, 3.96 and 1.00 us, and the clock stayed there until 28.6.

```profile
12.00:14.00 2.00, 1.09 (x10) 0.90 (x10) 1.64 (x11) 1.06 (x3) 0.00 (x0) 0.50 1.12 351
```

```profile
8.90 1.20 PE L413 MATMUL modc<-sc_bf,wm 128*128 128x1 bf16 x25 [2.55 <-DMA wm<-in_w_mod_dram]
...
12.91 1.34 PE L550 MATMUL wdp<-ident,wdn 128*128 128x128 bf16 x10 [2.00 <-DMA wdn<-in_B_w_down_dram]
```
